# Attention feeding a gated MLP on one core: transpose copies queued ahead of the first masks, mask template made behind the load requests, row sums one step forward

## The chip, the cores and the metric

One core of a Trainium2 chip. The metric is the device time of one execution in microseconds (us), the median of several; the profile gives the span of one profiled execution, some 1.5 to 2 us less. Single executions of one kernel differ mostly by about 0.3%.

Engines: PE (matrix engine), DVE (vector), ACT (scalar), POOL (issues the load requests here), SP (issues the other transfers). "Cold" and "warm" are the two speeds at which PE is seen here: four transposes of 96 columns take 0.37 us cold and 0.28 us warm.

## The reference

```python
# q, k, v: (8, 8, 576, 64) float32; batch, heads, positions, head size
scores = q @ k.T / 8 + slope[h] * -(i - j)        # only 0 <= i - j < 128, else -1e9
attn   = softmax(scores)
x      = (attn @ v) as (4608, 512)                 # batch x position, head x size
out    = (gelu(x @ w_gate) * (x @ w_val)) @ w_out  # 512 -> 1536 -> 512, float32
```

## The kernel before

A batch is 576 positions in five blocks, its eight heads four pairs (`c`). Queries and keys are transposed (`qT`, `kT`), multiplied into scores, exponentiated on ACT and multiplied by `emask` (the exponential of the bias, zero outside the window) on DVE. `sums` adds up the rows with a matmul against ones and takes the reciprocal on DVE; `spread_pe` brings the reciprocals to all partitions with a matmul; `values` multiplies by v and by the reciprocals into `xT`, the MLP's input. Groups of 512 positions then go through `gate_val` and `out_half`, and the attention of the next batches is strewn among the `out_half` steps by a list called `todo`. The parts that matter:

```python
    def scores(b, s, cs, then=None):
        pss = []
        for c in cs:
            ...                               # PE: the scores of pair c into two banks
        if then:
            sums(*then)
        for c, ps in zip(cs, pss):
            ...
            for i in (0, 1):
                exp(P[:, i, :], ps[i])        # ACT, L170
            mask(...)                         # DVE, L173

    def sums(b, s):
        ...                                   # PE, L221
        nc.vector.reciprocal(sumrow[b][:, lo:hi], ps[:, 0:hi - lo])   # DVE, L230

    def spread_pe(b, s):
        ...                                   # PE, L244: four spreads, two matmuls each
        for c, ps in enumerate(pss):
            copy = nc.scalar.copy if c % 2 == 0 else nc.vector.tensor_copy
            copy(out=recip[b][:, c, lo:hi], in_=ps[:, 0:hi - lo])     # L251
    ...
    load_runs(0, 0, 4)                        # POOL: requests for q and k, heads 0-3 (pairs 0, 1)
    ...                                       # identity
    nc.gpsimd.iota(tmpl, ...)                 # the mask template: iota, two selects
    ...
    load_runs(0, 4, 8)                        # heads 4-7 (pairs 2, 3)
    load_runs(1, 0, 8)                        # the remainders: positions 384-575, all heads
    ...                                       # v, weights; eight exponentials make emask

    act, dve = nc.scalar.copy, nc.vector.tensor_copy
    for cs in ((0, 1), (2, 3)):
        for w in (0, 1):                      # q, then k
            for c in cs:
                ps = bank().bitcast(BF16)
                transpose_runs(0, w, c, ps)                     # PE, L128
                untangle(act if c == 3 else dve, 0, w, c, ps)   # the copy, L136
        if cs[0] == 0:
            scores(0, 0, cs)
    scores2(0)                                # block 2 of all heads

    def rest(cs):                             # the remainders, copies on DVE
        ...
    rest((0, 1))
    scores(0, 0, (2, 3))
    rest((2, 3))
    scores(0, 1, (0, 1), (0, 0))
    scores(0, 1, (2, 3))
    spread_pe(0, 0)
    values(0, 0, range(4))
    sums(0, 1)
    for f in range(2):
        gate_val(0, f, 0, 320)                # the first gate matmuls, L281
    spread_pe(0, 1)
    ...
```

The transposes of batch 1 on PE (L142) come later, in the first gate stage; those of batches 2 and up are made by transfers.

The softmax here doesn't subtract the row's maximum and nothing guards it: scores larger than these inputs give would overflow.

## Time and profile before

| kernel before | |
|---|---|
| time, median of 3 (370.83 us of 4, below) | 370.61 us |
| span of the profiled execution | 368.8 us |
| PE busy | 351.2 us |
| first reciprocal (DVE L230) | 18.30 us |
| first gate matmul (PE L281) | 24.61 us |
| first transpose of batch 1 (PE L142) | 43.08 us |
| second spread of batches 1, 2, 3 (PE L244) | 67.89, 110.98, 146.46 us |

PE is nearly full, so the table gives times from the start of the span at which it reaches a known place. All kernels here end 222.3 us after the second spread of batch 3 (368.8 - 146.46), give or take 0.1, so a gain that is there at that place is there at the end. The prediction below shows the page's lines and the waits.

### The profile page before, as it was taken

The page shows a single profiled execution, that of the slowest core. Times are in us where ns is not written, and L with a number is a line of the kernel's source. Part 1 is how long each engine was busy: PE and PEld are TensorE (multiplying, and loading weights), DVE is VectorE, ACT ScalarE, POOL GpSimd, SP SyncE. Part 2 cuts the span into 40 slices and gives each one's busy share as a digit, 9 for nine tenths or more (in the row PEclk, how much of TensorE's full clock was granted, in tenths as well). Part 3 has the DMA queues.
Part 4 walks back from the last instruction along what each step waited for, and adds up shares of the span by engine and source line. Part 5 has one row for each costly group of instructions (what it writes and reads, how often), then busy time and mean ns, then how long its engine had stood idle before and what let it go on. Part 6 is the DMA issues. An engine that isn't in the chain of part 4 may idle for free.

```text
span 368.8 us, 6643 instructions
## 1 busy us (share of the span) xinstructions
PE 351.2 (95%) x2656; PEld 171.4 (46%) x2656; DVE 190.3 (52%) x310; ACT 186.9 (51%) x335; POOL 107.9 (29%) x140
## 2 busy tenths in 40 slices
PE   3789999999999999999999999999999999999995
PEld 2555544444444444444444444444444444444442
DVE  4795448544695459574556555745564504402420
ACT  5753478433966358753684268435943133323321
POOL 8936769905317401920660040000000000000000
PEclk9999999999999999999999999999999999999999
DMA  8999999999959994999994994096205020011002
GB/s 94 146 200 177 180 161 183 177 154 179 168 107 91 146 108 53 136 124 188 139 179 76 192 129 103 32 190 82 85 32 130 0 87 28 1 59 58 0 28 87
DMA packets 151168, 41.41 MB, mean 112 GB/s; under 512 B 138816, under 2 KB 144448, under 8 KB 151136
## 3 DMA queue, kind: packets, MB, share of 16 engines
q0 software_dynamic: 112608, 18.88, 67.4%
q1 hardware_dynamic: 38528, 22.10, 27.5%
q8 instruction: 21, 0.34, 0.4%
q14 instruction: 11, 0.09, 0.1%
HBM read 42.47 MB, written 9.51 MB: 141 GB/s over the span
## 4 chain that ended last, share of the span: by engine, by line
PE 85%; ACT 7%; DVE 5%; DMA 1%; issue 1%; POOL 0%; POOLq 0%; DVEq 0%; ACTq 0%
PE ps L281 50%; PE ps L297 23%; ACT P L170 6%; PE ps L163 4%; PE ps L262 4%; PE ps L221 2%; DVE r L230 2%; DVE P L173 2%; DMA ks<-in_k_dram 1%; PE ps L244 1%; DVE xT L268 1%; ACT L170 1%; PE ps L128 1%; PE ps L142 1%; ACT osb L302 0%
## 5 line engine op out<-in xcount | busy, mean ns | idle before, releaser
L286 DVE TENSOR_TENSOR hT<-ps,gelu 128x512 bf16<-128x512 f32 (+2 forms) x111 | 74.4, 674 | 121.6 <-PE ps L281 108.2
L285 ACT ACTIVATE gelu<-ps 128x512 bf16<-128x512 f32 (+2 forms) x111 | 64.9, 586 | 119.5 <-PE ps L281 119.3
L281 PE MATMUL ps<-xT,wg 128*128 128x512 bf16 (+2 forms) x444 | 112.2, 374 | 0.3
L281 PE MATMUL ps<-xT,wv 128*128 128x512 bf16 (+2 forms) x444 | 111.4, 373 | 0.0
L297 PE MATMUL ps<-wo,hT 128*128 128x512 bf16 x432 | 99.5, 380 | 0.0
L170 ACT ACTIVATE P<-ps 128x512 bf16<-128x512 f32 x144 | 74.5, 629 | 9.6 <-PE ps L163 9.5
L281 PEld LDWEIGHTS <-wv 128*128 128x128 bf16 x444 | 43.3, 98 | 50.5 <-issue 0.5
L173 DVE TENSOR_TENSOR P<-P,emask 128x1024 bf16<-128x1024 bf16 x72 | 48.6, 686 | 34.2 <-ACT P L170 33.9
L281 PEld LDWEIGHTS <-wg 128*128 128x128 bf16 x444 | 41.9, 98 | 48.7 <-issue 0.9
L297 PEld LDWEIGHTS <-hT 128*128 128x128 bf16 x432 | 39.5, 98 | 48.7 <-issue 4.1
L84 POOL DMA_DIRECT2D vb<-in_v_dram x40 | 33.7, 871 | 78.7 <-PE ps L262 78.5
L302 ACT COPY osb<-ps 128x512 f32<-128x512 f32 x36 | 21.7, 602 | 36.4 <-PE ps L297 31.9
L84 POOL DMA_DIRECT2D qs<-in_q_dram x35 | 29.6, 885 | 25.0 <-DMA qT<-qs 13.2
L230 DVE RECIPROCAL r<-ps 128x320 f32<-128x320 f32 (+1 forms) x16 | 30.7, 1938 | 2.8 <-PE ps L221 2.7
L84 POOL DMA_DIRECT2D ks<-in_k_dram x35 | 29.8, 898 | 6.7 <-DMA qs<-in_q_dram 3.8
L163 PE MATMUL ps<-qT,kT 64*128 64x256 bf16 (+1 forms) x384 | 24.6, 258 | 2.5 <-DVE kT L136 1.7
L268 DVE TENSOR_TENSOR xT<-ps,rb 128x320 bf16<-128x320 f32 (+1 forms) x64 | 24.7, 448 | 0.6 <-DMA rb<-rd 0.6
L163 PEld LDWEIGHTS <-kT 64*128 64x128 bf16 x384 | 13.5, 98 | 16.7 <-issue 12.2
L262 PE MATMUL ps<-P,vb 128*64 128x128 bf16 (+2 forms) x384 | 19.4, 251 | 0.1
L262 PEld LDWEIGHTS <-vb 128*64 128x64 bf16 x384 | 15.4, 113 | 7.3 <-issue 6.7
L221 PE MATMUL ps<-P,ones 128*32 128x128 bf16 (+2 forms) x384 | 10.9, 250 | 1.3 <-DVE P L173 1.1
L221 PEld LDWEIGHTS <-ones 128*32 128x32 bf16 x384 | 8.2, 99 | 5.7 <-issue 5.3
(47 smaller groups left out, 91.6 us busy)
## 6 DMA issues: line engine op xcount, KB each, us to landing
out_dram<-osb SPq DMA_DIRECT2D x36, 256.0 KB, 2.8
rb<-rd SPq DMA_DIRECT2D x8, 576.0 KB, 7.0
vb<-in_v_dram POOLq DMA_DIRECT2D x32, 128.0 KB, 4.8
qs<-in_q_dram POOLq DMA_DIRECT2D x28, 128.0 KB, 6.4
ks<-in_k_dram POOLq DMA_DIRECT2D x28, 128.0 KB, 6.2
wg<-in_moe_w_gate_dram POOLq DMA_DIRECT2D x4, 384.0 KB, 10.7
wv<-in_moe_w_val_dram POOLq DMA_DIRECT2D x4, 384.0 KB, 12.0
wo<-in_moe_w_out_dram POOLq DMA_DIRECT2D x2, 768.0 KB, 10.9
```

The source lines that it names most:

```text
L84: nc.gpsimd.dma_start(out=t[lo:128, j, :].rearrange("p (h d) -> p h d", h=H), in_=src[b][:, 128 * j - 64 + lo:128 * j + 64, :].rearrange(" ...
L163: nc.tensor.matmul(out=ps[:, col:col + 128 * n].rearrange("p (n t) -> p n t", n=n), lhsT=blocks(kT, b, i, c, j, 1).rearrange("p n t -> p ( ...
L170: nc.scalar.activation(out=dst, in_=src, func=AF.Exp, scale=0.125)
L173: nc.vector.tensor_tensor(out=dst, in0=dst, in1=m, op=ALU.mult)
L221: nc.tensor.matmul(out=ps[32 * c:32 * c + 32, a:e], lhsT=ones[:, min(j, 1), i, :], rhs=prob(b, s, c, i, j, e - a), start=(i == 0 and j == ...
L230: nc.vector.reciprocal(sumrow[b][:, lo:hi], ps[:, 0:hi - lo])
L262: nc.tensor.matmul(out=ps[64 * i:64 * i + 64, a:e], lhsT=vb[b % 2][:, j, 64 * h:64 * h + 64], rhs=prob(b, s, c, i, j, e - a), start=(j == ...
L268: nc.vector.tensor_tensor(out=xT[:, c, b * S + lo:b * S + hi], in0=ps[:, 0:hi - lo], in1=recip[b][:, c, lo:hi], op=ALU.mult)
L281: nc.tensor.matmul(out=ps[:, 0:hi - lo], lhsT=w[:, c, 128 * f:128 * (f + 1)], rhs=xT[:, c, t0 + lo:t0 + hi], start=(c == 0), stop=(c == 3))
L285: nc.scalar.activation(out=gl[:, 0:hi - lo], in_=pg[:, 0:hi - lo], func=AF.Gelu)
L286: nc.vector.tensor_tensor(out=hid[g][:, f, lo:hi], in0=pv[:, 0:hi - lo], in1=gl[:, 0:hi - lo], op=ALU.mult)
L297: nc.tensor.matmul(out=po, lhsT=hid[g][:, f, 128 * t:128 * (t + 1)], rhs=wo[:, f, :], start=(f == 0), stop=(f == NF - 1))
```

## The change

Its intent: DVE and ACT do their queued work in the order in which it was written (the prediction names its source and the trace's example, a copy at 11.49 us behind a mask that began at 10.42), so work that PE waits for should not stand behind work that it doesn't. (a) The requests for heads 4 to 7 go out before the mask template is made. (b) The copies of pair 2 are written before the first masks, and the scores of pairs 2 and 3 before the remainders. (c) The last four copies go to ACT, after the sums. (d) In `todo`, the sums of batches 1 to 3 stand earlier by one `out_half`, or ahead of masks. In that list "s" and "s2" are scores, "sum" is `sums`, "spread" `spread_pe`, "pv" `values`, and a number is an `out_half` step.

```diff
--- before.py
+++ after.py
@@ -196,7 +196,7 @@
                 for i in (0, 1):
                     score(b, c, i, j, qj, n, ps[i], col)
         if then:
-            sums(*then)
+            then()
         for c, ps in zip(cs, pss):
             P = p_pool[s].tile([128, 2, 512], BF16, name="P")
             probs[b, s, c] = P
@@ -312,6 +312,7 @@
     nc.gpsimd.affine_select(
         out=ident, in_=ident, compare_op=ALU.not_equal, fill=1.0,
         base=0, pattern=[[-1, 128]], channel_multiplier=1)
+    load_runs(0, 4, 8)
     tmpl = consts.tile([128, 256], FP32, name="tmpl")
     nc.gpsimd.iota(tmpl, pattern=[[1, 256]], base=0, channel_multiplier=-1,
                    allow_small_or_imprecise_dtypes=True)
@@ -320,7 +321,6 @@
         nc.gpsimd.affine_select(
             out=t, in_=t, compare_op=ALU.is_ge, fill=1e9,
             base=base, pattern=[[step, 128]], channel_multiplier=chan)
-    load_runs(0, 4, 8)
     load_runs(1, 0, 8)
     for c in range(4):
         nc.gpsimd.affine_select(
@@ -348,27 +348,27 @@
 
 
     act, dve = nc.scalar.copy, nc.vector.tensor_copy
-    for cs in ((0, 1), (2, 3)):
+    def first(cs):
         for w in (0, 1):
             for c in cs:
                 ps = bank().bitcast(BF16)
                 transpose_runs(0, w, c, ps)
                 untangle(act if c == 3 else dve, 0, w, c, ps)
-        if cs[0] == 0:
-            scores(0, 0, cs)
-    scores2(0)
-
-    def rest(cs):
+
+    def rest(cs, copy):
         for c in cs:
             for w in (0, 1):
                 ps = bank().bitcast(BF16)
                 transpose_runs(1, w, c, ps)
-                untangle(dve, 1, w, c, ps)
-
-    rest((0, 1))
-    scores(0, 0, (2, 3))
-    rest((2, 3))
-    scores(0, 1, (0, 1), (0, 0))
+                untangle(copy, 1, w, c, ps)
+
+    first((0, 1))
+    scores(0, 0, (0, 1), lambda: first((2,)))
+    first((3,))
+    scores2(0)
+    scores(0, 0, (2, 3), lambda: rest((0, 1), dve))
+    scores(0, 1, (0, 1), lambda: sums(0, 0))
+    rest((2, 3), act)
     scores(0, 1, (2, 3))
     spread_pe(0, 0)
     values(0, 0, range(4))
@@ -394,16 +394,17 @@
 
     todo = {
         0: [("s2", 1), ("s", 1, 0, (0, 1)), 0, ("s", 1, 0, (2, 3)), 1, 2,
-            ("s", 1, 1, (0, 1), (1, 0)), 3, ("s", 1, 1, (2, 3)), 4, ("spread", 1, 0),
-            ("pv", 1, 0), 5, ("sum", 1, 1), 6, ("spread", 1, 1), ("pv", 1, 1), 7],
+            ("s", 1, 1, (0, 1), lambda: sums(1, 0)), 3, ("s", 1, 1, (2, 3)), 4,
+            ("spread", 1, 0), ("pv", 1, 0), ("sum", 1, 1), 5, 6, ("spread", 1, 1),
+            ("pv", 1, 1), 7],
         1: [("s2", 2), ("s", 2, 0, (0, 1)), 0, ("s", 2, 0, (2, 3)), 1, 2,
-            ("s", 2, 1, (0, 1), (2, 0)), 3, ("s", 2, 1, (2, 3)), ("s2", 3), ("spread", 2, 0),
-            ("pv", 2, 0), 4, ("s", 3, 0, (0, 1)), 5, ("sum", 2, 1), 6, ("spread", 2, 1),
-            ("pv", 2, 1), ("s", 3, 0, (2, 3)), 7],
-        2: [("s", 3, 1, (0, 1), (3, 0)), 0, ("s", 3, 1, (2, 3)), 1, ("spread", 3, 0),
-            ("pv", 3, 0), ("s2", 4), 2, ("s", 4, 0, (0, 1), (3, 1)), 3, ("spread", 3, 1),
-            ("pv", 3, 1), 4, ("s", 4, 0, (2, 3)), 5, ("s", 4, 1, (0, 1)), 6, 7,
-            ("s", 4, 1, (2, 3))],
+            ("s", 2, 1, (0, 1), lambda: sums(2, 0)), 3, ("s", 2, 1, (2, 3)), ("s2", 3),
+            ("spread", 2, 0), ("pv", 2, 0), 4, ("sum", 2, 1), ("s", 3, 0, (0, 1)), 5, 6,
+            ("spread", 2, 1), ("pv", 2, 1), ("s", 3, 0, (2, 3)), 7],
+        2: [("s", 3, 1, (0, 1), lambda: sums(3, 0)), 0, ("s", 3, 1, (2, 3)), 1,
+            ("spread", 3, 0), ("pv", 3, 0), ("s2", 4), ("sum", 3, 1), 2,
+            ("s", 4, 0, (0, 1)), 3, ("spread", 3, 1), ("pv", 3, 1), 4, ("s", 4, 0, (2, 3)), 5,
+            ("s", 4, 1, (0, 1)), 6, 7, ("s", 4, 1, (2, 3))],
     }
 
     def steps(g):
```

## The prediction

> **What bounds the kernel now.** I read the page, then the waits of PE stage by stage, the chain that ended last, and the timelines of the stages with waits.
>
> ```profile
> PE 351.2 (95%) x2656; PEld 171.4 (46%) x2656; DVE 190.3 (52%) x310; ACT 186.9 (51%) x335; POOL 107.9 (29%) x140
> PE   3789999999999999999999999999999999999995
> ```
>
> PE is the bound: 351.2 of 368.8 us, and only the first three slices (9.2 us each) and the last fall below nine tenths. Idle PE time, 17.6 us in all, is all that a reordering can win. The table by stages puts about 9.4 us of it before 25 us, 4.3 us between 25 and 159 us, and the rest at the end of the kernel. Waits of PE, 0 to 25 us:
>
> ```profile
> PE ps L128 <- DMA qs<-in_q_dram: 4.9, 1, 4.9
> PE ps L163 <- DVE kT L136: 1.7, 2, 1.4
> PE ps L244 <- DVE r L230: 1.4, 1, 1.4
> ```
>
> The first wait is the first load and stays. The other two come from the opening's chain (start, duration, what):
>
> ```profile
> 8.33 2.06 ACT P L170 x4
> ...
> 10.42 0.69 DVE P L173
> 11.11 0.47 DVE qT L136
> 11.58 0.47 DVE kT L136
> 12.10 0.39 PE ps L163 x4
> ...
> 18.30 2.16 DVE r L230
> 20.46 2.29 DVE P L173 x4
> ```
>
> The copies of pair 2 (heads 4 and 5, L136) stand in DVE's order behind two masks (L173), and the second mask waits for ACT's exponentials. PE finished these transposes before 10.36 us, but scores2 got its data at 12.05. Everything up to the first reciprocal (18.30), and DVE's run of reciprocal, masks, copies and xT products to 25.2 us, hangs on that. Later the shape recurs: PE stands before the second spread of batches 1, 2 and 3 (PE's timeline):
>
> ```profile
> 67.89 0.71 PE L244 MATMUL ps<-r,sel 32*128 32x256 f32 x8 [0.46 <-DVE r L230]
> 110.98 0.71 PE L244 MATMUL ps<-r,sel 32*128 32x256 f32 x8 [0.97 <-DVE r L230]
> 146.46 0.71 PE L244 MATMUL ps<-r,sel 32*128 32x256 f32 x8 [0.47 <-DVE r L230]
> ```
>
> In the worst one the reciprocal was queued behind two masks of the next batch (DVE's timeline):
>
> ```profile
> 107.59 0.69 DVE L173 TENSOR_TENSOR P<-P,emask 128x1024 bf16<-128x1024 bf16 x1 [0.25 <-ACT P L170]
> 108.57 0.69 DVE L173 TENSOR_TENSOR P<-P,emask 128x1024 bf16<-128x1024 bf16 x1 [0.29 <-ACT P L170]
> 109.18 1.75 DVE L230 RECIPROCAL r<-ps 128x256 f32<-128x256 f32 x1
> ```
>
> The loads matter too. Per microsecond (last columns: DMA share, GB/s):
>
> ```profile
> 5.00:6.00 1.00, 0.77 (x12) 0.52 (x12) 0.52 (x2) 1.00 (x4) 1.00 (x2) 1.00 1.00 101
> 6.00:7.00 1.00, 0.51 (x10) 0.51 (x12) 0.51 (x2) 0.81 (x3) 1.00 (x2) 1.00 1.06 115
> 7.00:8.00 1.00, 0.67 (x12) 0.23 (x6) 0.94 (x2) 0.00 (x0) 0.88 (x3) 1.00 1.53 179
> ```
>
> Between the first and the second q/k requests the queue runs nearly dry; afterwards it is busy almost without a break to about 87 us.
>
> **What the Trainium skill says.** "PSUM — Partial Sum Buffer", Engine vs sequencer instructions: ScalarE and VectorE queues are strictly first in, first out. The trace agrees (the kT copy at 11.49 behind the mask that began at 10.42), and the whole argument rests on it. "ScalarE: Activation LUTs", What ACT_TABLE_LOAD costs: an ACTIVATE with immediate operands takes 186 ns + 0.833 ns per column; ACT's two 384-column copies here took 0.51 and 0.53 us against 0.506, so I estimate 0.35 us for 192 columns, as DVE takes. "DMA: Bandwidth & Descriptors", Two DMAs through the same engine are not ordered: descriptors of one queue start in order but are pipelined; here the requests landed in order (4.9, 6.4, 8.4, 9.5 us), so an earlier second q should not overtake the first k. "TensorE: Matmul & The Clock Gate", Single matmul latency: a cold matmul takes (219+N)/1.2 ns, a warm one (398+N)/2.4. The 128-column transposes of the opening took 313 ns against 289, later 128-column matmuls 219 against 219: the opening runs cold until about 23.6 us.
>
> **The change, part by part.** Nothing is added or removed; instructions move, and four 192-column copies go from DVE to ACT.
>
> (a) Template behind requests. q and k of heads 4-7 are issued at about 3.24 and 4.02 instead of 4.21 and 4.98. The mask template (iota and two selects, 0.99 us) ends at 5.7 instead of 4.2, so the eight emask exponentials (2.56 us) end at 8.3, just when the first scores are ready (8.32 before). Cost zero, but no slack. The dry spell fills: at 180 GB/s it lost about 0.12 MB, 0.7 us of the stream.
>
> (b) Copies ahead of masks. In built order PE does pair 2's q and k first, then pair 3's. From 8.68, six matmuls take 0.43 us and a copy starts 0.57 us after its first: DVE copies at 9.25 and 9.7, done 10.3. ACT copies pair 3 after its four exponentials, at 10.25 and 10.6, done 11.14 as before. That is the new limit for scores2: last two matmuls 11.2 instead of 12.1; its exponentials at 11.5 instead of 12.53, a gain of 1.05. scores(0,0,(2,3)) now follows directly, without waiting behind the remainders' transposes: ACT does P2 and these four without a gap, six at about 0.5: done 14.5 instead of 16.1. DVE: P2 mask 12.6-13.3, four copies (0.27 apart) to 14.35, masks to 14.95 and 15.55 (16.85 before). The sums start on the last mask at 15.6, need about 1.05 more cold, and the reciprocal starts at 16.7 instead of 18.30: **1.6 us**.
>
> (c) The last four copies on ACT, after the sums: PE transposes 16.65-17.65, ACT copies to 18.25, scores to 18.8, four exponentials to 20.4 (20.9 before). DVE: reciprocal to 18.8, four masks to 21.3, copies 0.88, xT 1.68: 23.7 instead of 25.2. The gate matmuls start **1.5 us** earlier; ACT trails DVE by only some tenths here, so little more can be won.
>
> (d) sums moved one out_half forward (1.40 us of PE work). Batch 1: the reciprocal already followed DVE's products (end 65.97, start 66.08): 0.15 us. Batch 2: it now starts at 107.3, ahead of the masks, and ends at 109.1, before PE wants it at 110.0: all 0.97. Batch 3: behind the P2 mask (end 144.2) it ends at 145.9, PE arrives at 146.0: 0.45. Sum **1.55 us**.
>
> Total 1.5 + 1.55 = 3.05 us: 370.6 becomes 367.5. I state 367.6, for small waits that I did not see.
>
> **Rivals.** (1) *Loads do not come forward.* The stream is DMA-bound, so it gains at most 0.7 us while PE gains 1.5. The last k of batch 1 lands at 41.2 (issued 35.5, 5.7 to landing), PE wants it at 43.3: 2.1 us of slack. The transposed q of batch 3 lands at 99.1 (88.05 + 11.1) and scores2(3) wants it at about 101.1, after the change at 99.4. That is within a few tenths; if the stream stays, 0.3 to 0.7 us come back as a wait: 368.1. (2) *The first k is slowed* by the q request now right behind it, or the template is late: ACT's first exponential has no slack, so each tenth is lost whole. For it: two requests in flight share 180 GB/s, where the tail of k alone had about 101. Against: in-order start. 0.5 us lost: 368.1; if 1 us, 368.6. (3) *ACT becomes the opening's bound*: it has four more copies and emask later, and its exponentials end only 0.9 us before DVE's masks do. If the copies cost 0.5 each, the chain grows 0.3: 367.9. (4) *More*: an opening with fewer gaps warms the PE clock before 20 us. The spread (1.45 cold, 0.82 later) and values (2.1, later 1.1) shrink, but DVE's products set the gate's start; at most 0.5: 367.1.
>
> **Range and chances.** All rivals together would still leave (d); all for the better, 366.6. Range 366.6 to 369.3. Two per cent is 7.4 us, more than twice the sum, and the removable idle before 25 us is about 4 us: faster 0.02. Nothing adds work: slower 0.01. The rest, 0.97, is "within 2%".
>
> **What would show it.** Right: first L230 at 16.5-17.0 us; first kT copy of pair 2 before the first mask; first L281 at 22.9-23.3; first exponential still at 8.3-8.4; waits before the second L244 of batches 2 and 3 below 0.1. PE's busy time stays near 351, the span loses 3. Wrong: first k transposes later than 6.6; a wait of L163 on a DMA transpose near 99 us; a new wait of L142 on ks near 42; idle DVE after 18.8 us for exponentials.

## The result, and the profile after

| | before | after |
|---|---|---|
| time, median of 4 | 370.83 us | 367.44 us (367.19 to 367.80) |
| span of the profiled execution | 368.8 us | 365.5 us |
| first reciprocal | 18.30 us | 16.61 us |
| first gate matmul | 24.61 us | 23.33 us |
| first transpose of batch 1 | 43.08 us | 41.70 us |
| second spread of batch 3 | 146.46 us | 143.21 us |

The ratio is 0.9907 (95% interval 0.9889 to 0.9925): less time, inside the two per cent. Ratios in this document are the mean time of one kernel's runs over that of the other's in the same rounds, so not quite the ratio of the medians quoted. Executions over 1.5% slower than the fastest of the same kernel are left out of the means. 367.6 had been predicted.

The page of the changed kernel, busy times and the rows of PE's busy share and of its recorded clock:

```profile
PE 347.8 (95%) x2614; PEld 171.3 (47%) x2656; DVE 188.6 (52%) x306; ACT 187.3 (51%) x339; POOL 107.9 (30%) x140
...
PE   3799999999999999999999999999999999999995
...
PEclk9779999999999999999999999999999999999999
```

PE's lower busy time can't be read as it stands: 42 of the 2656 matmul records are missing in this trace (the weight loads are all there). In the run without (c), below, whose trace is complete, it is 349.7 us. The row of the clock is taken up below.

PE's timeline of the opening, changed kernel (start, duration, what; in brackets the idle time before it and what ended it):

```profile
6.20 0.85 PE L128 MATMUL ps<-ident,ks 128*64 128x128 bf16 x12 [0.29 <-DMA ks<-in_k_dram]
7.39 1.07 PE L163 MATMUL ps<-qT,kT 64*128 64x256 bf16 x8 [0.34 <-DVE kT L136]
8.39 0.53 PE L128 MATMUL ps<-ident,qs 128*64 128x128 bf16 x6
8.85 0.53 PE L128 MATMUL ps<-ident,ks 128*64 128x128 bf16 x6
...
11.07 0.67 PE L163 MATMUL ps<-qT,kT 64*128 64x128 bf16 x10 [0.68 <-ACT kT L136]
```

DVE's timeline of the same stretch:

```profile
8.99 0.56 DVE L136 COPY qT<-ps 128x384 bf16<-128x384 bf16 x1 [1.20 <-PE ps L128]
9.46 0.55 DVE L136 COPY kT<-ps 128x384 bf16<-128x384 bf16 x1
9.93 1.28 DVE L173 TENSOR_TENSOR P<-P,emask 128x1024 bf16<-128x1024 bf16 x2
...
16.61 2.16 DVE L230 RECIPROCAL r<-ps 128x320 f32<-128x320 f32 x1 [1.21 <-PE ps L221]
```

And ACT's:

```profile
5.77 2.56 ACT L346 ACTIVATE emask<-tmpl 128x256 bf16<-128x256 f32 x8 [3.74 <-POOL tmpl L321]
8.24 2.03 ACT L170 ACTIVATE P<-ps 128x512 bf16<-128x512 f32 x4
...
11.33 5.11 ACT L170 ACTIVATE P<-ps 128x512 bf16<-128x512 f32 x10 [0.32 <-PE ps L163]
```

The copies of pair 2 now stand before the masks (9.46 against 9.93), PE waits for ACT's copies of pair 3 instead of DVE's, and ACT does block 2's two exponentials, the four of pairs 2 and 3 and the next four in one unbroken run of ten. The template's place on POOL shows in ACT's first line: `emask` ends just when the first scores' exponentials begin. It holds them up a little: they start 0.85 us after their scores (7.39 to 8.24), where 0.64 is enough before (7.68 to 8.32).

PE's lines of the second spread of batches 1, 2 and 3, changed kernel:

```profile
66.30 0.71 PE L244 MATMUL ps<-r,sel 32*128 32x256 f32 x8 [0.34 <-DVE r L230]
...
108.25 0.71 PE L244 MATMUL ps<-r,sel 32*128 32x256 f32 x8
...
143.21 0.71 PE L244 MATMUL ps<-r,sel 32*128 32x256 f32 x8
```

The waits of batches 2 and 3 (0.97 and 0.47 us before) are gone, batch 1's is 0.34 instead of 0.46. In batch 2 the reciprocal stands ahead of the masks, as DVE's timeline shows:

```profile
104.07 1.68 DVE L268 TENSOR_TENSOR xT<-ps,rb 128x320 bf16<-128x320 f32 x4
105.66 1.75 DVE L230 RECIPROCAL r<-ps 128x256 f32<-128x256 f32 x1
107.33 1.23 DVE L173 TENSOR_TENSOR P<-P,emask 128x1024 bf16<-128x1024 bf16 x2
```

### The profile page after: what moved, and what is told of

The parts are those of the page before. It is cut to its first block, busy times and chain, and to the rows that moved or that the text cites. A ratio compares the mean times of both kernels' runs of the same rounds, so it can differ in the third digit from the quotient of the medians.

```text
span 365.5 us, 6601 instructions
## 1 busy us (share of the span) xinstructions
PE 347.8 (95%) x2614; PEld 171.3 (47%) x2656; DVE 188.6 (52%) x306; ACT 187.3 (51%) x339; POOL 107.9 (30%) x140
## 3 DMA queue, kind: packets, MB, share of 16 engines
HBM read 42.47 MB, written 9.51 MB: 142 GB/s over the span
## 4 chain that ended last, share of the span: by engine, by line
PE 86%; ACT 5%; DVE 3%; DMA 3%; issue 1%; POOL 1%; POOLq 0%; SPq 0%; ACTq 0%; DVEq 0%
PE ps L281 50%; PE ps L297 23%; PE ps L262 4%; ACT P L170 4%; PE ps L163 4%; DMA qT<-qs 3%; PE ps L221 2%; PE ps L244 2%; DVE r L230 1%; DVE P L173 1%; DVE xT L268 1%; ACT emask L346 1%; PE ps L142 1%; POOL ks L104 0%; ACT L170 0%
## 5 line engine op out<-in xcount | busy, mean ns | idle before, releaser
L281 PE MATMUL ps<-xT,wg 128*128 128x512 bf16 (+2 forms) x430 | 110.6, 374 | 0.8
L297 PE MATMUL ps<-wo,hT 128*128 128x512 bf16 x413 | 97.2, 380 | 1.5 <-issue 0.6
L170 ACT ACTIVATE P<-ps 128x512 bf16<-128x512 f32 x144 | 74.4, 632 | 7.1 <-PE ps L163 7.0
L281 PEld LDWEIGHTS <-wg 128*128 128x128 bf16 x444 | 41.9, 98 | 48.9 <-issue 1.1
L163 PE MATMUL ps<-qT,kT 64*128 64x256 bf16 (+1 forms) x384 | 24.0, 254 | 3.0 <-DVE kT L136 1.3
L163 PEld LDWEIGHTS <-kT 64*128 64x128 bf16 x384 | 13.1, 96 | 16.9 <-issue 11.6
```

The costliest lines, as they stand in the source:

```text
L163: nc.tensor.matmul(out=ps[:, col:col + 128 * n].rearrange("p (n t) -> p n t", n=n), lhsT=blocks(kT, b, i, c, j, 1).rearrange("p n t -> p ( ...
L170: nc.scalar.activation(out=dst, in_=src, func=AF.Exp, scale=0.125)
L281: nc.tensor.matmul(out=ps[:, 0:hi - lo], lhsT=w[:, c, 128 * f:128 * (f + 1)], rhs=xT[:, c, t0 + lo:t0 + hi], start=(c == 0), stop=(c == 3))
L297: nc.tensor.matmul(out=po, lhsT=hid[g][:, f, 128 * t:128 * (t + 1)], rhs=wo[:, f, :], start=(f == 0), stop=(f == NF - 1))
```

## The experiments

The theory: the gain is the sum of two independent parts, an opening shortened because DVE and ACT are strictly in order, (a) to (c), and waits taken out of batches 1 to 3, (d). The rivals: the parts feed each other; (a) is worth nothing; the gain hangs on PE's clock; the loads don't follow.

One table serves all runs. Each profiled execution is cut at four places: first transposes of k on PE ("k"), first reciprocal ("r"), first transpose of batch 1 ("t"), second spread of batch 3 ("e"). The four stretches add up to the place of e.

| run | k | k to r | r to t | t to e | e | median time (us) | ratio |
|---|---|---|---|---|---|---|---|
| before | 6.49 | 11.81 | 24.78 | 103.38 | 146.46 | 370.83 | 1 |
| after | 6.20 | 10.41 | 25.09 | 101.51 | 143.21 | 367.44 | 0.9907 |
| a2_after_again | 6.38 | 10.30 | 25.62 | 101.50 | 143.80 | 367.78 | 0.9909 |
| e1_sums_only | 6.32 | 12.35 | 24.92 | 101.51 | 145.10 | 368.83 | 0.9952 |
| e10_opening_only | 7.30 | 10.31 | 24.77 | 103.37 | 145.75 | 369.34 | 0.9960 |
| e2_order_only | 6.47 | 10.57 | 25.67 | 103.38 | 146.09 | 369.96 | 0.9982 |
| e3_no_template_move | 6.39 | 11.18 | 25.40 | 101.51 | 144.48 | 368.25 | 0.9939 |
| e4_no_late_rest | 6.81 | 10.31 | 24.77 | 101.51 | 143.40 | 367.59 | 0.9926 |
| e5_pair2_only | 6.54 | 11.61 | 25.06 | 103.37 | 146.58 | 370.20 | 0.9983 |
| e6_template_only | 6.51 | 11.60 | 24.77 | 103.37 | 146.25 | 370.33 | 0.9994 |
| e7_warm_pe | 6.39 | 9.85 | 24.77 | 101.97 | 142.98 | 367.07 | 0.9889 |
| e11_warm_no_template | 6.24 | 11.44 | 24.77 | 101.51 | 143.96 | 368.83 | 0.9941 |
| e8_act_spread | 6.62 | 10.31 | 24.55 | 101.05 | 142.53 | 366.63 | 0.9882 |
| e9_warm_act_spread | 6.30 | 10.25 | 23.98 | 101.58 | 142.11 | 366.25 | 0.9868 |

Ratios are to the kernel before in the same rounds, whose medians were 370.47 to 371.17 there. All results were correct. t to e repeats to 0.01 us wherever `todo` and the code behind t are the same and no load is late; k is where a load happens to land, and not one kernel's property alone.

### The two halves

**The sums alone** (kernel before with the changed kernel's `todo` and nothing else; `then` is a function now, so that the sums can be named there):

```diff
-            ("s", 1, 1, (0, 1), (1, 0)), 3, ("s", 1, 1, (2, 3)), 4, ("spread", 1, 0),
-            ("pv", 1, 0), 5, ("sum", 1, 1), 6, ("spread", 1, 1), ("pv", 1, 1), 7],
+            ("s", 1, 1, (0, 1), lambda: sums(1, 0)), 3, ("s", 1, 1, (2, 3)), 4,
+            ("spread", 1, 0), ("pv", 1, 0), ("sum", 1, 1), 5, 6, ("spread", 1, 1),
+            ("pv", 1, 1), 7],
 ...            # likewise for batches 2 and 3, as in the change
```

> The kernel before with only the later sums moved one out_half forward (part d); opening untouched. My theory: opening as before (first L244 at 20.6, first L281 at 24.6), and the gain is what the two traces show at the three second spreads, 0.21 + 1.14 + 0.52 = 1.87 us: span 366.9, time about 368.9, ratio 0.995. Rival, that the sums come early enough only because the opening runs ahead or the DVE order undoes it: span above 368.3.

Measured: 0.9952 (0.9938 to 0.9965); t to e falls from 103.38 to 101.51, by 1.87 us. Its unchanged opening was slower in this profile: PE waited 0.53 us more for the k of a remainder (13.15 us), so e gained only 1.36 there.

**The opening alone** (the changed kernel with the old `todo`; the functions again only carry the sums):

```diff
-            ("pv", 1, 0), ("sum", 1, 1), 5, 6, ("spread", 1, 1), ("pv", 1, 1), 7],
+            ("pv", 1, 0), 5, ("sum", 1, 1), 6, ("spread", 1, 1), ("pv", 1, 1), 7],
 ...            # likewise for batches 2 and 3
```

> The changed kernel with the sums of batches 1 to 3 put back where they were; the opening (template behind the requests, copies of pair 2 ahead of the masks, score matmuls ahead of the remainders, last copies on the scalar engine) stays changed. It is the other half of the run of the sums alone, which measured 1.87 us between the first transposes on the tensor engine for batch 1 and the second spread of batch 3. If the two halves add up, this stretch takes 103.4 us here as in the kernel before (101.5 in the changed one), the waits for the reciprocal in batches 1 to 3 (0.46, 0.97, 0.47 us) are back, the first reciprocal comes at 16.6 us and the time falls by 1.1 to 1.6 us, to 0.996 to 0.997 of the kernel before. If an earlier opening changes these waits too, the stretch differs from 103.4 by over 0.3 us.

Measured: 0.9960 (0.9944 to 0.9977), t to e 103.37 us. PE's lines of the three second spreads in this run:

```profile
67.19 0.71 PE L244 MATMUL ps<-r,sel 32*128 32x256 f32 x8 [0.47 <-DVE r L230]
...
110.28 0.71 PE L244 MATMUL ps<-r,sel 32*128 32x256 f32 x8 [0.97 <-DVE r L230]
...
145.75 0.71 PE L244 MATMUL ps<-r,sel 32*128 32x256 f32 x8 [0.46 <-DVE r L230]
```

All three waits are back to within a hundredth, though everything comes 0.7 us earlier. The halves are independent: t to e is that of the kernel before, and within the noise 0.48% and 0.40% add up, to 0.88%, where the whole change measured 0.93% and 0.91%. The first reciprocal, expected at 16.6, came at 17.61, because the first k landed late:

```profile
7.30 0.85 PE L128 MATMUL ps<-ident,ks 128*64 128x128 bf16 x12 [1.54 <-DMA ks<-in_k_dram]
```

From k to r it took 10.31, as in the changed kernel. So the opening is a chain that hangs on the landing of the first k, and the landing moves from run to run.

### Which part of the opening

**Order alone**: kernel before with (b), and the last remainder's copies on DVE ahead of the sums; no (a), no (d).

```diff
-    for cs in ((0, 1), (2, 3)):
-        ...
-    scores2(0)
-    rest((0, 1))
-    scores(0, 0, (2, 3))
-    rest((2, 3))
-    scores(0, 1, (0, 1), (0, 0))
+    first((0, 1))
+    scores(0, 0, (0, 1), lambda: first((2,)))
+    first((3,))
+    scores2(0)
+    scores(0, 0, (2, 3), lambda: rest((0, 1), dve))
+    rest((2, 3), dve)
+    scores(0, 1, (0, 1), lambda: sums(0, 0))
```

> The kernel before with only the opening's order changed (part b: pair 2's copies ahead of the first masks, scores of pairs 2 and 3 ahead of the remainders); template still ahead of the second requests, last remainders on DVE and ahead of the sums. My theory: the FIFO order is the cause, the loads are not; second k lands near 9.5, so 0.3 us less than in the full change: first L230 at 16.9 to 17.1, first L281 at 23.6 to 23.8, gain 1.1, time about 369.6. Rival, that the earlier requests make the gain: first L230 stays near 18, gain below 0.4.

Measured: 0.9982 (0.9969 to 0.9994). The reciprocal came at 17.04 as expected, but only 0.37 us of the 1.26 are left at e: r to t took 25.67 us instead of 24.78. What that is comes below, under the clock. In the time the expectation missed: 0.7 us (0.18%) instead of 1.1.

**The copies of pair 2 alone**: scores of pairs 2 and 3 stay behind the remainders.

```diff
+    first((0, 1))
+    scores(0, 0, (0, 1), lambda: first((2,)))
+    first((3,))
     scores2(0)
     rest((0, 1), dve)
     scores(0, 0, (2, 3))
     rest((2, 3), dve)
```

> The kernel before with one thing changed: the copies of the k and q transposes of head pair 2 are queued on the vector engine ahead of the first two masks (as in the changed kernel), but the score matmuls of heads 2 and 3 stay behind the remainders of the pairs before, the mask template stays ahead of the requests, and the sums stay where they were. If the copies' place in the vector engine's queue is what the opening's gain comes from, the first reciprocal (18.30 us in the kernel before) comes at about 17.4 us and the time falls by 0.5 to 0.9 us, to 0.998 of the kernel before. If it is the place of the score matmuls instead, the reciprocal stays at 18.2 to 18.4 us and the time stays within 0.2 us of the kernel before. With the template still ahead of the requests I expect the tensor engine to wait for the second head's k at about 9.6 us, as in the run of the order alone.

Measured: 0.9983 (0.9965 to 1.0002): the interval holds 1 as well as the 0.998 of the first theory, so the times don't decide. The reciprocal came at 18.15, beside the 18.2 to 18.4 of the rival and far from the 17.4 of the theory. ACT's timeline tells where the gain went, and PE's line what took it:

```profile
11.95 1.08 ACT L170 ACTIVATE P<-ps 128x512 bf16<-128x512 f32 x2 [0.38 <-PE ps L163]
13.90 2.06 ACT L170 ACTIVATE P<-ps 128x512 bf16<-128x512 f32 x4 [0.87 <-PE ps L163]
...
12.64 0.37 PE L128 MATMUL ps<-ident,ks 96*64 96x96 bf16 x4 [0.42 <-DMA ks<-in_k_dram]
```

Block 2's exponentials come 0.58 us earlier than before (12.53), but then ACT waits 0.87 us for the scores of pairs 2 and 3, which PE does only after the transposes of the remainders, one of which waits 0.42 us for its k. What was won in front is lost in this gap: these scores start at 13.26 us, hardly earlier than before (13.42). So it is a load, and not only the scores' place, that stood in the way. The transposes follow each other by 0.16 us, so with this k in time the scores would have come some 0.6 us earlier, an estimate from this trace (12.02 instead of 12.64); a run with the copies alone and the k in time was not made. Shown is that the copies alone gave 0.15 us here, and that in the new order the scores' place takes these scores out of the way of that load.

**Template alone**:

```diff
+    load_runs(0, 4, 8)
     tmpl = consts.tile([128, 256], FP32, name="tmpl")
     ...
-    load_runs(0, 4, 8)
     load_runs(1, 0, 8)
```

> The kernel before with the mask template made behind the requests for q and k of heads 4 to 7, and nothing else. The changed kernel with this part undone lost 1.3 us of span, so the part is worth about 1 us beside the new order. If it is worth this only because the new order asks for k of heads 4 to 7 earlier, then alone it is worth almost nothing: these transposes are copied when the masks ahead of the copies let them, the first reciprocal stays within 18.0 to 18.4 us (18.30 in the kernel before) and the time within 0.3 us of the kernel before. If the earlier requests are worth it by themselves, the first reciprocal comes at about 17.3 us and the time falls by 0.7 to 1.0 us.

Measured: 0.9994 (0.9976 to 1.0011), reciprocal at 18.11. Alone it is worth nothing that shows.

**The changed kernel without (a)**: the same edit backwards.

> The changed kernel with the template back ahead of the second requests (part a undone). My theory: first k lands at 6.45 again instead of 6.20 and the second k near 9.5 instead of 8.85; both have slack because ACT's emask then ends at 6.8; loss 0.2 to 0.4 us: first L230 at 16.8 to 17.0, time about 367.8. Rival (loads carry the opening's gain): first L230 at 17.5 or later, time 368.5.

Measured: 0.9939 (0.9926 to 0.9951), against 0.9907 and 0.9909 of the changed kernel, a loss of about 1.1 us. A miss: 0.2 to 0.4 was expected, and the reciprocal came where the rival had it, at 17.57 us. PE's line of the second k, without (a):

```profile
10.15 0.53 PE L128 MATMUL ps<-ident,ks 128*64 128x128 bf16 x6 [1.00 <-DMA ks<-in_k_dram]
```

Against 8.85 without a wait in the changed kernel. The exponentials that follow start at 12.28 instead of 11.33, and reciprocal and first gate matmul come 0.96 us later each. In the order-alone run PE had this k at 9.63 us; in both, the reciprocal follows it by 7.4 us (17.04 - 9.63, 17.57 - 10.15). The old order asks for the second k last, at 9.51, and its DVE is not free before, so it hardly noticed; the new order asks for it right after the second q and so needs the earlier request. That earlier request is visible on POOL. Before:

```profile
3.24 0.37 POOL L316 IOTA tmpl<- 128x256 f32 x1
3.69 0.54 POOL L320 TENSOR_SCALAR_AFFINE_SELECT tmpl<-tmpl 128x128 f32<-128x128 f32 x2
4.21 0.78 POOL L104 DMA_DIRECT2D qs<-in_q_dram  x1
4.98 0.75 POOL L104 DMA_DIRECT2D ks<-in_k_dram  x1
```

After:

```profile
3.23 0.78 POOL L104 DMA_DIRECT2D qs<-in_q_dram  x1
4.00 0.76 POOL L104 DMA_DIRECT2D ks<-in_k_dram  x1
4.75 0.38 POOL L317 IOTA tmpl<- 128x256 f32 x1
```

**The changed kernel without (c)**: the last copies on DVE, ahead of the sums.

```diff
     scores(0, 0, (2, 3), lambda: rest((0, 1), dve))
+    rest((2, 3), dve)
     scores(0, 1, (0, 1), lambda: sums(0, 0))
-    rest((2, 3), act)
```

> The changed kernel with the last remainders back ahead of the sums and their four copies on DVE (part c undone). My theory: these copies fall between the masks (end 15.4) and the reciprocal (16.6) where DVE idles 1.2 us, so nothing is lost: first L230 within 0.2 of 16.6, first L281 within 0.2 of 23.3, time 367.2 to 367.7. Rival, that the copies on DVE hold up masks or reciprocal: first L230 at 17.2 or later, time 368.2 or more.

Measured: 0.9926 (0.9914 to 0.9939) and a median 0.15 us above the changed kernel's; k to r 10.31. The four copies run at 15.83 to 16.98 us, in DVE's idle time before the reciprocal, so (c) takes nothing off the chain. Its interval overlaps those of the changed kernel.

### The clock of PE

**The changed kernel once more**, unchanged, beside the next three.

> The changed kernel once more, to see how far the first k's landing (6.20 in its first profile, 6.81 in the kernel that differs only after it) and the moment the PE clock turns warm vary. Theory: first k lands between 6.2 and 6.8; ACT's first exponential follows it (8.24 to 8.65) and everything to the first L244 shifts with it; span 365.2 to 366.0, ratio 0.990 to 0.993. Rival, that the landing doesn't vary and the other kernel's 6.81 had a cause of its own: 6.20 again within 0.05.

Measured: 0.9909 (0.9894 to 0.9924). The profiled span is 366.1, 0.6 us more than the first time. PE's timeline of the first gate matmuls, first profile:

```profile
23.33 0.83 PE L281 MATMUL ps<-xT,wg 128*128 128x320 bf16 x4
24.00 0.71 PE L281 MATMUL ps<-xT,wv 128*128 128x320 bf16 x4
```

and in the second:

```profile
23.40 1.25 PE L281 MATMUL ps<-xT,wg 128*128 128x320 bf16 x4
24.44 0.87 PE L281 MATMUL ps<-xT,wv 128*128 128x320 bf16 x4
```

Same kernel, same order, start within 0.07 us, yet these eight matmuls take 1.75 us instead of 1.22 to the start of the next: the clock turned warm about a microsecond later. That is what the column "r to t" measures. Where PE is warm in time it is 24.77 us, in five runs to the hundredth (24.78 in the kernel before); there the first gate matmuls are paced by DVE's products, for which PE is seen waiting 0.69 us in three of the five. Where PE stays cold it is up to 25.67. The changed kernel lost 0.32 us to this in its first profile and 0.85 in its second.

**PE kept busy**: zero matmuls into banks that are overwritten anyway, placed where PE waits, 38 in all.

```diff
+    def fill(ps, n, cols=128):
+        for _ in range(n):
+            nc.tensor.matmul(out=ps[:, 0:cols], lhsT=qs[1][0:64, 0, 0:128],
+                             rhs=qs[1][0:64, 0, 0:cols], start=True, stop=True)
 ...
             for i in (0, 1):
                 score(b, c, i, 2, 2, 1, ps[i], 128 * c)       # in scores2
+            if b == 0 and c == 3:
+                fill(ps[0][:, 384:512], 8)
 ...
             ps = [bank(), bank()]                             # in scores
+            if b == 0 and c < 2:
+                fill(ps[0], ((4, 2), (14, 2))[s][c])
 ...
                 ps = bank()                                   # in first
+                if c == 0:
+                    fill(ps, (7, 1)[w], 512)
```

> The changed kernel with matmuls of zeros put on PE where it waits in the opening, into banks that the next real matmul overwrites (7 of 512 columns before the first q, then some 30 of 128 columns), to keep its clock warm. Theory A (cold matmuls sit on the path only where PE sets the gate's start: values 2.13, second sums 1.04): spread 0.82, values 1.18, sums 0.62 and the first L281 at 22.8 to 23.0, set by DVE's xT products; gain 0.3 to 0.5 us over the change, span 365.1. Rival B: the opening is wholly DVE's and ACT's, gain below 0.1. Rival C: the clock stays cold or the fillers stand in the way: span 365.5 or more.

Measured: 0.9889 (0.9873 to 0.9905). PE is warm from about 10.6 us, the spread takes 0.82 us, the first gate matmul comes at 22.08 (22.8 to 23.0 had been expected) and t at 41.01, 0.69 us earlier than in the first profile of the changed kernel. But t to e is 0.46 us longer. PE's line (the added code moves the line numbers by nine or more from here on; lines up to L178, so L142, L163 and L170, keep theirs):

```profile
41.97 0.23 PE L142 MATMUL ps<-ident,ks 128*128 128x128 bf16 x1 [0.30 <-DMA ks<-in_k_dram]
```

PE comes to batch 1's transposes 2.07 us earlier than in the kernel before (41.01 against 43.08), and the last k, for which the prediction had read 2.1 us of slack and a landing at 41.2, is there only at about 41.9. The 0.23 us that are left of the 0.69 are what e shows.

**The same without (a)**, to ask what the template's place is worth at equal clock:

> The changed kernel with zero matmuls in the tensor engine's waits (the run that kept its clock up: first reciprocal 16.24, first gate matmul 22.08, first transpose of batch 1 at 41.01 us, 367.07 us) and with the mask template ahead of the requests for heads 4 to 7 again. It asks what the template's place is worth when the moment at which the clock rises is the same in both. If the place of the requests sets when k of heads 4 to 7 lands, the tensor engine waits for that k at about 9.6 to 10.1 us, the first reciprocal comes at 16.7 to 17.2 us, and the first gate matmul 0.4 to 1.0 us later than 22.08; the time is 367.4 to 368.1 us. If most of the 1.3 us that the changed kernel lost without the move was the cold clock of that run, the first gate matmul is within 0.3 us of 22.08 and the time within 0.3 us of 367.07.

Measured: 0.9941 (0.9920 to 0.9962), 367.22 to 369.44 in six runs, the widest scatter of all. Reciprocal at 17.68 us, 1.44 later than with (a). It does not answer its question cleanly: the clock was not equal. PE stayed cold up to about 18 us (four transposes of a remainder took 0.37 us instead of 0.28), and twelve of the fill matmuls, cold, held up the scores for the exponentials ahead of the sums. Block 2's exponentials, ahead of that, come at 12.02 against 11.42 us, but half of these 0.6 us is the clock as well: PE had the second k at 9.42 against 9.10 us, 0.3 later. Beside the run of both together (below), whose fill matmuls ahead of these exponentials are as cold (311 ns each in both), they come 0.29 later (12.02 against 11.73). From k to r, order alone lost 0.26 and the run without (a) 0.87 us against the 10.31 of the changed order. I put (a) at 0.3 to 0.9 us at the reciprocal beside the new order; how much it is hangs on when the second k lands.

### A better version

In the floor of 24.77 us it is DVE that sets the pace: reciprocal, masks, two copies of the first spread, products. So the **two DVE copies of each first spread were put on ACT**:

```diff
-            copy = nc.scalar.copy if c % 2 == 0 else nc.vector.tensor_copy
+            copy = nc.scalar.copy if s == 0 or c % 2 == 0 else nc.vector.tensor_copy
```

> The changed kernel with all four copies of the first spreads (rb, 320 columns) on ACT, so that DVE's run of reciprocal, masks, copies, products loses 0.88 us. Theory: in the opening DVE's products end 0.8 earlier (22.7), but PE's cold values and second sums end at 23.4 and now set the gate alone: first L281 at 23.2 to 23.4, gain 0 to 0.1 there; before the second spread of batch 1 the wait of 0.34 goes: gain 0.4 in all, span 365.1. Rival: ACT's longer copies delay the products: span 365.5 or more.

Measured: 0.9882 (0.9866 to 0.9897). r to t is 24.55 though the spread was cold, and t to e is 101.05: batch 1's wait is gone too. A part of the gain over the changed kernel of the same rounds (0.9909) is the clock's and not the copies': here the second sums ran warm (0.62 us, there 1.04). Against the floor of 24.77 the copies give 0.22 us, and 0.46 behind t.

**Both together** (this and the busy PE):

> Both together: a warm PE and DVE relieved of the copies. Theory: each alone is stopped by the other engine in the opening, together the first L281 comes at 22.1 to 22.5, 0.8 to 1.2 us earlier than in the change, and the wait of batch 1 goes: gain 1.3, span 364.2, time 366.1. Rival: something else, ACT's emask and exponentials, holds the opening: gain 0.6 or less, span 364.9 or more.

Measured: 0.9868 (0.9853 to 0.9884), median 366.25 us, the best of all; beside the changed kernel in the same rounds (367.57 to 367.90 against 365.96 to 366.54) the ratio of the means is 0.9959. r to t is 23.98, yet t to e is 101.58, 0.53 longer than with the copies on ACT alone. PE's timeline shows two waits for loads behind t:

```profile
41.55 0.23 PE L142 MATMUL ps<-ident,ks 128*128 128x128 bf16 x1 [0.35 <-DMA ks<-in_k_dram]
...
89.37 0.84 PE L163 MATMUL ps<-qT,kT 64*128 64x128 bf16 x16 [0.31 <-DMA qT<-qs]
```

The first is the last k of batch 1, which the prediction had named as a next limit. The second is a transposed q too, but that of batch 2, whose scores open this group's `todo`; the prediction had named batch 3's, wanted near 99 us. Further shortening of the opening has to bring both forward.

## Why the prediction was right

The time (367.6, measured 367.44), the range and the class held. By its steps:

- **(a) Template behind the requests: "Cost zero", and no gain of its own. Mis-sized both ways.** "No slack" was right, and the cost was not zero where k landed early: the first exponential waited 0.2 us for `emask` (0.85 us after its scores instead of 0.64), and k to r is 10.41 in that profile against 10.31 in three where k came later. The gain was larger: the schedule of (b), "From 8.68, six matmuls take 0.43 us", presumed the second k there, and I had taken its landing from a kernel that asked for it at 9.51. Without (a) it came at 9.4 to 10.15 us in four runs, and the changed kernel lost 1.1 us of time. So (a) carries 0.3 to 0.9 of the 1.6 us booked under (b). The sum was right, its division wrong.
- **(b) Copies ahead of masks: 1.6 us at the reciprocal. Right**: 1.69, of which 0.29 is a first k that landed earlier and 1.40 the order (k to r, 11.81 to 10.41). I had named the copies as the cause; alone they gave 0.15, with a late load in the way. The request's place alone gives nothing that shows. Copies and scores' place together, without it, gave 1.26 at the reciprocal in one run and 0.73 in the other; the scores' place alone was not run.
- **(c) Last copies on ACT: little. Right**: nothing measurable. The gate matmuls came at 23.33 (22.9 to 23.3 predicted): 1.28 earlier instead of 1.5. Not (c) is to blame but the clock: the second sums ran cold, 1.04 us against 0.62 before. At the transposes of batch 1 it is 1.38.
- **(d) Sums forward: 1.55. Mechanism right, size 0.32 short**: 1.87. By batch, from the second spreads: 0.21 (0.15 predicted), 1.14 (0.97), 0.52 (0.45). The gain of batch 2 is above its shown wait. A part of this is how the wait is counted: six `out_half` matmuls show 1.47 us, but with no wait behind them PE starts the next thing after 1.42 (143.68 to 145.10 us in the run of the sums alone), so a shown wait of 0.47 is 0.52. The other tenth is the order itself: steps 5 and 6, between which the sums stood, now follow each other, and their twelve matmuls take 2.69 us (105.56 to 108.25), where before each step took 1.40 (106.59 to 107.99).
- **Sum 3.05; measured 3.25 in the span**, 1.38 + 1.87. The two errors have opposite signs. That the number came so close is partly luck: 0.29 us of the gain is where a load happened to land in this profile, and 0.32 went to the clock.
- **Rival 1, loads:** not in the changed kernel (its trace puts 0.16 us at 97.82 down to a transposed q, but ahead of an `out_half`, which reads none and one of whose six records is missing; the second profile has no such wait). As soon as the opening shrinks further two loads are there, 0.3 us each in the best version, one of them another than the prediction named. A third, the k of a remainder, it had not looked at: PE waited 0.29 to 0.53 us for it in four of the experiments.
- **Rival 2, first k slowed:** not decided. In the eight profiles with the request right behind it, k is transposed at 6.20 to 7.30 us (mean 6.56), in the six without at 6.24 to 6.54 (mean 6.41). The difference of the means is small; the late ones (6.62, 6.81, 7.30) are all on the side of the rival. The page quoted against it speaks of one queue of one engine and adds that nothing orders transfers across the 16 engines, so it gave less cover than the prediction took from it.
- **Rival 3, ACT as the bound:** no. Its four small copies took 0.32 to 0.35 us as estimated.
- **Rival 4, the clock:** a real one, but with the sign that I hadn't considered. I took it as a gain of up to 0.5; in the changed kernel it was a loss of 0.32 to 0.85 us against the floor of 24.77, since the gate matmuls came earlier than the warm clock. The filled kernel gained 0.69 at t.

## What to carry to other kernels

A strict order on an engine makes parts of a change depend on each other: ask of every instruction brought forward what it needs next, and whether that has been brought forward too; a load that "has slack" has it only against the old order. When a gain of a microsecond is at issue, cut the span at a few fixed places and compare stretches instead of ends; here one stretch repeated to 0.01 us while the landing of a load and the moment at which PE's clock rises moved the whole by a microsecond. And an opening that is shortened may run ahead of the clock: what was paced by DVE is then paced by a cold PE.

## What the Trainium skill lacked or had wrong

- "TensorE: Matmul & The Clock Gate", Part 1: The HAM clock gate, says that the moment at which the clock rises varies by half a microsecond either way because the activity window runs freely. The same kernel's first eight gate matmuls took 1.22 or 1.75 us, the rise being about a microsecond apart. That a freely running window is the reason no run here shows. The page puts the cost of the ramp at under 1% of a typical kernel's span, which holds here: 24.77 to 25.67 us from the first reciprocal to batch 1's transposes, 0.9 of 368.8 us. What it lacks is a warning that this is as large as a quarter of a change of one per cent, and that it differs between two profiles of one kernel.
- It also warns that the recorded clock events are unreliable, and the trace agrees. The form it took here: ahead of the first recorded change (at about 13.4 us in the changed kernel's profile) the record reads full speed, though PE is cold there. The kernel before from 14 to 17 us (last columns: recorded clock, transfer share, GB/s):

```profile
14.00:17.00 3.00, 2.48 (x34) 1.58 (x29) 2.84 (x8) 2.61 (x6) 3.00 (x5) 1.00 1.70 134
```

  and the changed kernel:

```profile
14.00:17.00 3.00, 2.72 (x50) 1.74 (x46) 1.79 (x4) 2.52 (x6) 3.00 (x5) 0.50 1.70 135
```

  Four transposes of 96 columns take 0.37 us in both. Durations decide, and the sevens in the changed kernel's row of the clock are no slower clock than before.
- No page that I read (the place would be "DMA: Bandwidth & Descriptors") says how far the landing of a load moves from run to run with the same requests ahead of it. With the next request right behind it, the first k was there at 6.20 to 7.30 us.
